# A fused gated-attention and rational-MLP kernel: the decay product of k moved to GpSimd, with a new order of work

## The chip, the cores and the metric

The kernel runs on one core of a Trainium2 chip. The core has a matrix engine (TensorE, PE in the profile, with its weight loads shown as PEld), VectorE (DVE), ScalarE (ACT), GpSimd (POOL) and a queue engine (SyncE, SP) that here only starts transfers. The engines run side by side, each through its own list of instructions in order, and wait for one another on semaphores. The metric is the time of one execution on the device, in microseconds (us); the median of several runs counts, and lower is better.

## The reference

Two stages follow each other. The first is a linear attention with a decay for each channel: a 48 x 48 state for each of 4 x 8 heads, over 768 steps. The second is an MLP whose nonlinearity is a rational function.

```python
def _attn_ref(q, k, v, f_logit):            # each (4, 8, 768, 48)
    f = 1.0 / (1.0 + np.exp(-f_logit))
    for t in range(S):
        state = f[:, :, t, :, None] * state + np.einsum('bhd,bhe->bhde', k[:, :, t], v[:, :, t])
        y[:, :, t] = np.einsum('bhd,bhde->bhe', q[:, :, t], state)

def _moe_ref(x, w_in, w_out, a, b):         # x (3072, 384), w_in (384, 2048), w_out (2048, 384)
    h = x @ w_in
    P = a[0] + a[1] * h + a[2] * h2 + a[3] * h3
    Q = 1.0 + np.abs(b[0]) * np.abs(h) + np.abs(b[1]) * h2
    return (P / (Q + 1e-06)) @ w_out
```

## The kernel before

The work is cut into 12 units, 256 tokens of one batch entry each: unit n takes token chunk n // 4 of batch entry n % 4. A unit passes through both stages. Nothing loops over the units in the code: one long string, `ORDER` (line 20), lists every step by a short name with its unit and its part, and the last loop of the kernel (L486) issues the steps in just that order. Since each engine runs its own instructions in the order in which they are issued, the string is the order of every engine's list. An `@` gives one of four PSUM slots to a step.

The steps of the attention, with the engine that runs each:

- `ld` loads f, k or q on SP's queue, v on GpSimd's (L114). `ef` and `ls` (ACT, L190 and L195) make the logarithm of the gate from f; `cs` (PE) sums it over the tokens of a piece; `A n x` (ACT, L221) exponentiates the sum, with x = 1 for k and x = 0 for q.
- `xa n x` (DVE, L227) is the decay product: k (x = 1) or q (x = 0) in fp32 times that factor, written as bf16 into the tile qkp. There are two qkp tiles, for units in turn. 128 partitions by 768 elements, all three operands in SBUF.
- `T` (PE) transposes both halves of qkp, and `Te` copies the result from PSUM to qkT: on ACT with an `s` behind it (L249), else on DVE (L251). `sc` (PE) makes the scores, `mk` (DVE, L272) multiplies them from PSUM with the mask.
- `vm` (GpSimd, L279) copies two strips of v, 128 elements a partition each. `kv`, `si` and `ae` make the new state in PSUM, `st` (DVE, L359) scales it from PSUM into SBUF. `yi` and `yb` (PE) make the output y, `ye` (ACT, L349) takes it to SBUF for the MLP. `kv` reads k's half of qkp too.

The steps of the MLP, on tiles of 16 blocks of 256 columns, often in halves (`0 8`, `8 16`) or quarters:

- `h` (PE, L368) multiplies with w_in, `hy` (ACT, L382) takes the result to SBUF. `sq` squares it (DVE, L386; `sa` is the same on ACT from PSUM), `ab` takes the absolute value into z (DVE, L394).
- Square and absolute value are added in one of three ways: on PE by `u` into PSUM, with the logarithm `ln` (ACT, L407) from there; in z on DVE by `zv` (L412); or in z by `zd`, a transfer that adds, issued on GpSimd's queue (L416). After `zv` and `zd` the logarithm is `lz` (ACT, L420). `ex` (ACT, L424) turns it into the reciprocal of Q.
- `p1`, `p2`, `pm` (DVE, L428, L433, L442) make the parts of P, added by `tv` on DVE (L450) or by `ta`, again a transfer that adds (GpSimd's queue, L446). `gm` (DVE, L454) multiplies with the reciprocal.
- `o` (PE, L462) multiplies with w_out, `oe` (ACT, the last one on DVE, L469) copies from PSUM, `so` stores on SP's queue. `wi` and `wo` load w_in and w_out in four slabs each on GpSimd's queue (L118, L124); `dz` are matmuls without use that fill PE's waits at the head.

`behind(i, mark)` (L477) makes an instruction wait for an earlier step that the dictionary `marks` holds by name.

Of the kernel before, what the change touches and what calls it, by code (L numbers as in the profile page):

```python
# [29 lines left out]
def kernel(  # L30
# [12 lines left out]
    nc = tc.nc  # L43
# [3 lines left out]
    HP = H // 2  # L47
# [14 lines left out]
    ld = ctx.enter_context(tc.tile_pool(name="ld", bufs=3))  # L62
# [30 lines left out]
    marks = {}  # L93

    def unit(n):
        if n not in units:
            c, b = divmod(n, B)
            units[n] = dict(c=c, b=b, qk=qkp[n % 2], ls=lsp[n % 2], vm=vmp[n % 2], st=states[b])
        return units[n]

    def slot(i, shape, dtype, name):
        return slots[i].tile(shape, dtype, name=name, tag="s")
# [114 lines left out]
    def A(n, x, a0=0, a1=HP):  # L217
        s = unit(n)
        t = A_sb[:, :, x, 2 * D * a0:2 * D * a1]
        src = s["cs", a0][:, :, 0:2 * D * (a1 - a0)]  # L220
        nc.scalar.activation(t, src, AF.Exp, scale=1.0 if x else -1.0)  # L221

    def xa(n, x, *args):
        s = unit(n)
        a0, a1 = args or (0, HP)
        hh = slice(2 * a0, 2 * a1)
        return nc.vector.tensor_mul(  # L227
            s["qk"][:, :, x, hh, 0:D],
            s["qk"[x]][:, hh].rearrange("p h i d -> p i h d"),
            A_sb[:, :, x].rearrange("p i (h d) -> p i h d", h=H)[:, :, hh])  # L230

    def T(n, *args):
        s = unit(n)
        a0, a1, sl = args if len(args) == 3 else (0, HP, args[0])
        t = s["tp", a0] = slot(sl, [P, 2, 2, HP, P], BF16, "tp")
        for x in (1, 0):
            for i in range(2):
                for p in range(a0, a1):
                    nc.tensor.transpose(t[:, x, i, p, :],  # L239
                                        s["qk"][:, i, x, 2 * p:2 * p + 2, :].rearrange("t h d -> t (h d)"), ident)  # L240

    def Te(n, *args):
        a0, a1 = [x for x in args if x != "s"] or (0, HP)
        s = unit(n)
        if "T" not in s:
            s["T"] = at.tile([P, 2, 2, HP, P], BF16, name="qkT")
        d, t = s["T"][:, :, :, a0:a1], s["tp", a0][:, :, :, a0:a1]
        if "s" in args:
            return nc.scalar.copy(d.bitcast(F32).rearrange("p x i a t -> p (x i) (a t)"),  # L249
                                  t.bitcast(F32).rearrange("p x i a t -> p (x i) (a t)"))  # L250
        return nc.vector.tensor_copy(d.rearrange("p x i a t -> p (x i) (a t)"),  # L251
                                     t.rearrange("p x i a t -> p (x i) (a t)"))
# [224 lines left out]
    def behind(i, mark):  # L477
        tc.add_manual_dep(i.ins, marks[mark].ins.name,
                          mybir.DependencyInfo(mybir.DependencyClass.Sync, mybir.DependencyReason.DATA),
                          reason="begins behind it")  # L480

    steps = dict(ld=load, wi=load_w_in, wo=load_w_out, ab_=load_ab, cu=const_u, ci=const_i, cm=const_m,
                 cz=const_z, fa=coef_a, fb=coef_b, fr=coef_r, ef=ef, ls=ls, cs=cs, A=A, xa=xa, T=T, Te=Te,
                 sc=sc, mk=mk, vm=vm, yi=yi, yb=yb, kv=kv, si=si, ye=ye, ae=ae, st=st, h=h, hy=hy, sq=sq, ab=ab, u=u, ln=ln,
                 zv=zv, zd=zd, sa=sa, lz=lz, ex=ex, p1=p1, p2=p2, pm=pm, ta=ta, tv=tv, gm=gm, o=o, oe=oe, so=store, dz=dz)
    for step in ORDER.replace("\n", ";").split(";"):  # L486
        if step.strip():
            name, *args = step.split()
            marks[".".join([name] + [x for x in args if x.isdigit()])] = steps[name](
                *(int(x.lstrip("@")) if x.lstrip("@").isdigit() else x for x in args))  # L490


# [1 line left out]
_INS = ['q', 'k', 'v', 'f_logit', 'moe_w_in', 'moe_w_out', 'moe_a', 'moe_b']  # L494
_OUTS = [((3072, 384), 'float32')]


# [23 lines left out]
```

## Time and profile before

| | us |
|---|---|
| median of 3 runs | 219.55 |
| the runs | 219.2, 221.58, 219.55 |
| the profiled execution | 218.93 |
| its span in the trace | 217.2 |

The profile shows one execution. Its span runs from the first instruction to the last; the execution's own time is a little longer than that. The page gives each engine's busy time and share of the span, the chain of work that ended last (followed back from the end, at each step to what released it), and groups of instructions by line, with the busy time and the mean length in ns of one behind a bar. A tile's name in a row is that of the program, with output before input. Further views, which the prediction quotes: busy time by stretches of the span, single instructions in order of time, and transfers by size with the time from issue to landing.

### The profile page before, as it was taken

Reading aid. Unit: us, or ns where it says so; the run is one execution under the profiler, and the core shown is the slowest. Engines: PE = TensorE matmul, PEld = TensorE weight load, DVE = VectorE, ACT = ScalarE, POOL = GpSimd, SP = SyncE. Lnnn points to the kernel's source line nnn. Section 1 sums busy time; section 2 is a strip of 40 time slices with the busy share of each in tenths; the row PEclk is TensorE's granted clock in tenths of the full one; section 3 lists DMA queues with packets and bytes.
Section 4 is the critical chain, followed back from the end, with each engine's and each line's share of the span. In section 5 each row is a group of like instructions: output and inputs, shape, how many; then the busy total and the mean of one; then the engine's idle time right before and its main releaser. Section 6 shows DMA issues by size and latency. Waiting matters only on the chain.

```text
span 217.2 us, 7159 instructions
## 1 busy us (share of the span) xinstructions
PE 203.3 (94%) x3164; PEld 140.2 (65%) x3171; DVE 202.9 (93%) x247; ACT 199.7 (92%) x209; POOL 90.2 (42%) x91
## 2 busy tenths in 40 slices
PE   6998989799799999999989999999999999999992
PEld 2456648458377658658758658668678577686551
DVE  4596999999999999999999999999999999999991
ACT  4734999999999999999999999999999999999990
POOL 5250072968146802014954205954332525433300
PEclk9999999999999999999999999999999999999999
DMA  5999999999897999958999997999789794999853
GB/s 141 244 228 206 216 249 203 204 251 213 122 240 145 236 232 279 150 100 195 196 232 214 210 250 182 181 231 219 152 170 227 140 155 83 174 185 189 157 213 145
DMA packets 60910, 42.13 MB, mean 194 GB/s; under 512 B 51152, under 2 KB 54992, under 8 KB 60880
## 3 DMA queue, kind: packets, MB, share of 16 engines
q0 software_dynamic: 21232, 22.81, 65.6%
q1 hardware_dynamic: 39360, 18.68, 34.0%
q8 instruction: 24, 0.39, 0.7%
q10 hardware_dynamic: 288, 0.20, 0.3%
q14 instruction: 6, 0.05, 0.1%
HBM read 25.17 MB, written 4.72 MB: 138 GB/s over the span
## 4 chain that ended last, share of the span: by engine, by line
DVE 36%; ACT 32%; DMA 15%; issue 7%; PE 7%; POOL 1%; POOLq 0%; DVEq 0%; ACTq 0%
ACT qi L424 8%; ACT hy L382 8%; ACT lq L420 6%; DVE h L386 6%; DVE scm L272 5%; DVE gall L454 5%; DMA w_in_sb<-in_moe_w_in_dram 4%; DMA kn<-in_k_dram 4%; DVE gall L442 4%; DVE z L394 3%; DVE qkp L227 3%; DVE gall L428 3%; DMA vn<-in_v_dram 3%; DMA z<-h 3%; DVE hy L433 3%
## 5 line engine op out<-in xcount | busy, mean ns | idle before, releaser
L462 PE MATMUL op<-w_out_sb,gall 128*128 128x384 bf16 x384 | 70.1, 326 | 0.4 <-ACT hy L382 0.4
L368 PE MATMUL hp<-xT,w_in_sb 128*128 128x256 bf16 x576 | 66.6, 273 | 1.6 <-ACT xT L349 0.9
L368 PEld LDWEIGHTS <-w_in_sb 128*128 128x128 bf16 x576 | 56.0, 98 | 11.8 <-issue 2.6
L279 POOL COPY vmp<-vn 128x128 bf16<-128x128 bf16 x24 | 41.9, 1758 | 31.8 <-DMA vn<-in_v_dram 27.8
L462 PEld LDWEIGHTS <-gall 128*128 128x128 bf16 x384 | 35.5, 98 | 23.7 <-DVE gall L454 1.0
L382 ACT CAST hy<-hp 128x1024 bf16<-128x1024 f32 x48 | 47.4, 1076 | 2.9 <-PE hp L368 2.9
L424 ACT ACTIVATE qi<-lq 128x2048 bf16<-128x2048 f32 (+1 forms) x26 | 46.9, 1845 | 0.0
L420 ACT ACTIVATE lq<-z 128x2048 f32<-128x2048 bf16 (+1 forms) x20 | 37.2, 1859 | 0.5 <-DMA z<-h 0.5
L446 POOL DMA_DIRECT2D gall<-hy x17 | 14.8, 925 | 50.6 <-PE hp L368 18.4
L416 POOL DMA_DIRECT2D z<-h x18 | 17.6, 1080 | 30.2 <-issue 10.4
L386 DVE TENSOR_TENSOR h<-hy 128x2048 bf16<-128x2048 bf16 (+1 forms) x26 | 27.3, 1059 | 2.7 <-ACT hy L382 2.7
L454 DVE TENSOR_TENSOR gall<-gall,qi 128x2048 bf16<-128x2048 bf16 (+1 forms) x26 | 29.4, 1139 | 0.2
L442 DVE TENSOR_TENSOR gall<-gall,h 128x2048 bf16<-128x2048 bf16 (+1 forms) x26 | 29.3, 1137 | 0.0
L272 DVE TENSOR_TENSOR scm<-sc,mask 128x1024 bf16<-128x1024 f32 x24 | 28.4, 1214 | 0.0
L221 ACT ACTIVATE A<-cs 128x768 f32<-128x768 f32 (+1 forms) x26 | 19.5, 813 | 0.4 <-DVE qkp L227 0.4
L394 DVE TENSOR_SCALAR z<-hy 128x2048 uint16<-128x2048 uint16 (+1 forms) x28 | 17.3, 625 | 0.2 <-ACT hy L382 0.2
L428 DVE TENSOR_SCALAR gall<-hy,a_sb 128x4096 bf16<-128x4096 bf16 (+1 forms) x14 | 17.1, 1218 | 0.0
L433 DVE TENSOR_SCALAR hy<-hy,a_sb 128x4096 bf16<-128x4096 bf16 (+1 forms) x14 | 16.6, 1187 | 0.0
L114 POOL DMA_DIRECT2D vn<-in_v_dram x12 | 14.1, 1175 | 0.7 <-PE y L286 0.7
L227 DVE TENSOR_TENSOR qkp<-kn,A 128x768 bf16<-128x768 f32 (+1 forms) x13 | 11.5, 888 | 1.9 <-ACT A L221 1.9
L349 ACT ACTIVATE xT<-y 128x768 bf16<-128x768 f32 x12 | 10.4, 868 | 3.0 <-PE y L286 3.0
L239 PE MATMUL tp<-ident,qkp 128*128 128x128 bf16 x192 | 12.8, 219 | 0.2
(70 smaller groups left out, 258.7 us busy)
## 6 DMA issues: line engine op xcount, KB each, us to landing
gall<-hy POOLq DMA_DIRECT2D x16, 512.0 KB, 6.6
z<-h POOLq DMA_DIRECT2D x15, 512.0 KB, 7.3
fn<-in_f_logit_dram SPq DMA_DIRECT2D x11, 384.0 KB, 8.9
kn<-in_k_dram SPq DMA_DIRECT2D x11, 384.0 KB, 9.5
qn<-in_q_dram SPq DMA_DIRECT2D x11, 384.0 KB, 6.8
out_dram<-osb SPq DMA_DIRECT2D x11, 384.0 KB, 4.2
vn<-in_v_dram POOLq DMA_DIRECT2D x12, 192.0 KB, 7.6
w_in_sb<-in_moe_w_in_dram POOLq DMA_DIRECT2D x4, 384.0 KB, 10.1
```

The source lines that it names most:

```text
L272: return nc.vector.tensor_mul(t, s["sc", g].rearrange("s r a i t -> s (r a) (i t)"), mb)
L279: nc.gpsimd.tensor_copy(s["vm"][:, :, :, 32 * x:32 * x + 16], src)
L368: nc.tensor.matmul(t[:, m - m0, :], w_in_sb[:, kk, m * P:(m + 1) * P], s["x"][:, kk].rearrange("p i j t -> p (i j t)"), start=(kk == 0), s ...
L382: nc.scalar.copy(fl(big(s, "hy", "hy", 3), m0, m1), fl(s["hp", m0], 0, m1 - m0))
L386: return nc.vector.tensor_mul(fl(big(s, "h2", "h2", 2), m0, m1), fl(s["hy"], m0, m1), fl(s["hy"], m0, m1))
L394: return nc.vector.tensor_scalar(fl(big(s, "z", "z", 2), m0, m1).bitcast(U16), fl(s["hy"], m0, m1).bitcast(U16), 0x7FFF, None, op0=ALU.bit ...
L420: nc.scalar.activation(fl(lq, m0, m1), fl(s["z"], m0, m1), AF.Ln, scale=regs[2], bias=1.0 + 1e-6)
L424: nc.scalar.activation(fl(qi, m0, m1), fl(lq, m0, m1), AF.Exp, scale=-1.0)
L428: return nc.vector.tensor_scalar(fl(big(s, "g", "gall", 3), m0, m1), fl(s["hy"], m0, m1), a_sb[:, 3:4], a_sb[:, 2:3], op0=ALU.mult, op1=AL ...
L442: return nc.vector.tensor_mul(fl(s["g"], m0, m1), fl(s["g"], m0, m1), fl(s["h2"], m0, m1))
L454: return nc.vector.tensor_mul(fl(s["g"], m0, m1), fl(s["g"], m0, m1), fl(qi, m0, m1))
L462: nc.tensor.matmul(s["op"][:, j, 0:DM], s["g"][:, m, P * j:P * j + P], w_out_sb[:, m, :], start=(s["on", j] == 1), stop=(s["on", j] == KF))
```

## The change

Three things are changed.

First, `xa` can run on GpSimd: with a `p` behind it, the product is the same multiplication on GpSimd instead of DVE, and is made to begin behind the mark `wide`. The loop that issues the steps sets that mark to the last DVE instruction so far of the kinds `sq`, `ab`, `p1`, `p2`, `pm`, `gm`, `zv`, `tv` and `xa`; these read and write SBUF alone.

```diff
     def xa(n, x, *args):
         s = unit(n)
-        a0, a1 = args or (0, HP)
+        pool = "p" in args
+        a0, a1 = [y for y in args if y != "p"] or (0, HP)
         hh = slice(2 * a0, 2 * a1)
-        return nc.vector.tensor_mul(
+        i = (nc.gpsimd if pool else nc.vector).tensor_mul(
             s["qk"][:, :, x, hh, 0:D],
             s["qk"[x]][:, hh].rearrange("p h i d -> p i h d"),
             A_sb[:, :, x].rearrange("p i (h d) -> p i h d", h=H)[:, :, hh])
+        if pool:
+            behind(i, "wide")
+        return i
...
     for step in ORDER.replace("\n", ";").split(";"):
         if step.strip():
             name, *args = step.split()
-            marks[".".join([name] + [x for x in args if x.isdigit()])] = steps[name](
+            i = marks[".".join([name] + [x for x in args if x.isdigit()])] = steps[name](
                 *(int(x.lstrip("@")) if x.lstrip("@").isdigit() else x for x in args))
+            if name in ("sq", "ab", "p1", "p2", "pm", "gm", "zv", "tv") or name == "xa" and "p" not in args:
+                marks["wide"] = i
```

Second, the whole `ORDER` is another one. The nine k products of units 3 to 11 (`xa 3 1` to `xa 11 1`) carry the `p`. Some steps take another form; all else is the same set of steps:

| step | before | after |
|---|---|---|
| k products on DVE / GpSimd (units 3 to 11) | 9 / 0 | 0 / 9 |
| `Te` of units 5 and 9 | ACT | DVE |
| `u` with `ln` (PE sum, quarters) | 11 | 3 |
| `zv` halves / quarters | 2 / 0 | 5 / 2 |
| `lz` halves / quarters | 17 / 3 | 20 / 5 |
| `zd` halves / quarters | 15 / 3 | 15 / 3 |
| `tv` halves / quarters | 6 / 3 | 6 / 2 |
| `ta` halves / quarters | 16 / 1 | 16 / 2 |
| warming matmuls (`dz`) | 31 | 24 |

With unit 0's two half copies, four `Te` steps now run on DVE.

Third, all steps stand in another place. At the head, q and k of unit 0 are loaded ahead of f of unit 1 and of v; the decay products of unit 0 begin with q; the exponentials and logarithms of units 1 and 2 stand between the steps of unit 0; w_in's slabs come from the first to the last. The nine products stand where DVE's list has masks and states next. The list around four of them, in the new order (each excerpt is a part of the one long line):

```
p1 1 0 16; ae 2; A 3 1; st 2 0; sc 2 1 @2; sc 2 0 @1; zd 1 8 16; A 3 0; ls 4; si 2 1; xa 3 1 p; mk 2 0; ex 0 8 16; yb 2 0 2 @0; yi 2 1; mk 2 1; yb 2 2 4; xa 3 0; vm 3 0; st 2 1; cs 4 @1; ye 2 s; wo 0 4; wo 4 8; T 3 @2
...
zv 2 0 8; mk 4 1; xa 5 1 p; ef 6; ae 4; o 1 0 8 12; mk 4 0; si 4 0; st 4 0; o 1 0 4 8; ld 7 q; lz 2 0 8; ex 2 0 8; o 1 1 8 12; gm 2 8 16
...
sq 6 8 16; xa 8 1 p; mk 7 1; st 7 0; lz 5 8 16; ex 5 8 16; o 4 1 8 12; mk 7 0; o 4 1 0 4; ld 10 k; ab 6 8 16
...
xa 11 0; mk 10 0; lz 8 0 8; mk 10 1; o 7 1 8 12; xa 11 1 p; vm 10 1; kv 10 @1; ab 9 8 16
```

At the tail the copy `oe 9` stands behind the last `ex`, and the stores of units 6, 7 and 8 are issued together.

2 lines of the change are left out of this document (1 added, 1 removed).

## The prediction

> **What bounds the kernel now.** I read the page's totals first, then the chain that ended last.
>
> ```profile
> span 217.2 us, 7159 instructions
> ...
> PE 203.3 (94%) x3164; PEld 140.2 (65%) x3171; DVE 202.9 (93%) x247; ACT 199.7 (92%) x209; POOL 90.2 (42%) x91
> ...
> DVE 36%; ACT 32%; DMA 15%; issue 7%; PE 7%; POOL 1%; POOLq 0%; DVEq 0%; ACTq 0%
> ```
>
> Three engines are busy for over 90% of the span, but the chain runs through VectorE (DVE) and ScalarE (ACT): 36% and 32%, with 7% on TensorE (PE). So work taken off PE alone is worth little. The busy times in stretches of 10 us come next (columns: stretch, length, then busy time and instructions of PE, PE's weight loads, DVE, ACT and GpSimd, the granted clock, DMA share, GB/s).
>
> ```profile
> 0.00:10.00 10.00, 8.02 (x32) 3.23 (x33) 4.75 (x28) 6.38 (x11) 3.88 (x15) 1.00 0.96 187
> 10.00:20.00 10.00, 8.95 (x195) 5.40 (x194) 7.98 (x14) 3.48 (x5) 3.78 (x6) 1.00 1.22 222
> 20.00:30.00 10.00, 9.89 (x193) 7.12 (x194) 8.97 (x13) 8.78 (x11) 2.16 (x4) 1.00 1.26 227
> ...
> 210.00:217.20 7.20, 3.14 (x19) 1.40 (x16) 2.06 (x4) 1.97 (x3) 0.00 (x0) 1.00 0.29 109
> sum 217.20, PE 203.29 PEld 140.16 DVE 202.89 ACT 199.68 POOL 90.18; mean PE 9.24 PEld 6.37 DVE 9.22 ACT 9.08 POOL 4.10
> ```
>
> DVE idles 217.20 - 202.89 = 14.3 us: 5.25 + 2.02 + 1.03 = 8.3 in the first 30 us, 7.20 - 2.06 = 5.1 in the last stretch, and so only 0.9 in the 180 us between. ACT idles 17.5, of which 3.62 + 6.52 + 1.22 = 11.4 at the head, 5.2 at the tail, 0.9 between. In the middle both are full: a microsecond of DVE work saved there shows in the end only if ACT gives up as much, and a stall of either shows whole. The clock is 1.00 in every row.
>
> **The change, part by part.** The rows for each kind of instruction (busy time and mean ns of one behind the bar):
>
> ```profile
> L420 ACT ACTIVATE lq<-z 128x2048 f32<-128x2048 bf16 x17 | 33.8, 1991 | 0.5 <-DMA z<-h 0.5
> L272 DVE TENSOR_TENSOR scm<-sc,mask 128x1024 bf16<-128x1024 f32 x24 | 28.4, 1214 | 0.0
> ...
> L249 ACT COPY qkT<-tp 128x1024 f32<-128x1024 f32 x11 | 11.9, 1077 | 0.0
> ...
> L407 ACT ACTIVATE lq<-u 128x1024 f32<-128x1024 f32 x11 | 11.2, 1041 | 0.0
> L359 DVE TENSOR_TENSOR state<-sv,alast 128x384 bf16<-128x384 f32 x20 | 11.0, 548 | 0.1
> ...
> L227 DVE TENSOR_TENSOR qkp<-kn,A 128x768 bf16<-128x768 f32 x11 | 10.4, 948 | 0.0
> ...
> L402 PE MATMUL u<-z,ident 128*128 128x512 bf16 x22 | 6.5, 379 | 0.4
> ...
> L420 ACT ACTIVATE lq<-z 128x1024 f32<-128x1024 bf16 x3 | 3.3, 1108 | 0.0
> ...
> L412 DVE TENSOR_TENSOR z<-z,h 128x2048 bf16<-128x2048 bf16 x2 | 2.4, 1220 | 0.0
> L450 DVE TENSOR_TENSOR gall<-gall,hy 128x1024 bf16<-128x1024 bf16 x3 | 2.1, 685 | 0.0
> ...
> L251 DVE COPY qkT<-tp 128x1024 bf16<-128x1024 bf16 x2 | 1.3, 687 | 0.0
> ```
>
> and of single instructions in order of time (start, length), first DVE's, then ACT's last ones:
>
> ```profile
> 13.47 2.36 DVE L272 TENSOR_TENSOR scm<-sc,mask 128x1024 bf16<-128x1024 f32 x2
> ...
> 45.14 1.33 DVE L428 TENSOR_SCALAR gall<-hy,a_sb 128x4096 bf16<-128x4096 bf16 x1
> 46.39 1.21 DVE L454 TENSOR_TENSOR gall<-gall,qi 128x2048 bf16<-128x2048 bf16 x1
> 47.52 0.95 DVE L227 TENSOR_TENSOR qkp<-kn,A 128x768 bf16<-128x768 f32 x1
> ...
> 51.53 1.34 DVE L433 TENSOR_SCALAR hy<-hy,a_sb 128x4096 bf16<-128x4096 bf16 x1
> ...
> 69.38 0.68 DVE L394 TENSOR_SCALAR z<-hy 128x2048 uint16<-128x2048 uint16 x1
> ...
> 71.42 0.94 DVE L394 TENSOR_SCALAR z<-hy 128x2048 uint16<-128x2048 uint16 x1 [0.22 <-ACT hy L382]
> ```
>
> ```profile
> 209.75 1.06 ACT L424 ACTIVATE qi<-lq 128x1024 bf16<-128x1024 f32 x1
> 210.71 0.78 ACT L469 COPY osb<-op 128x768 f32<-128x768 f32 x1
> 213.18 0.48 ACT L469 COPY osb<-op 128x384 f32<-128x384 f32 x1 [1.69 <-PE op L462]
> ```
>
> *DVE.* Nine k products (units 3 to 11, L227) leave: 9 x 0.948 = 8.53 us. The new order also reassigns other work. Two full copies of qkT (units 5 and 9) come over from ACT; the row is for half the size (0.687), so one costs between 1.22 (a 2048-element DVE row, L412) and 2 x 0.687 = 1.37; I take 1.30, as the source is that row's: 2.60. Additions of z on DVE (L412) go from two of 2048 to five of 2048 and two of 1024: 3 x 1.220 + 2 x 0.685 = 5.03 (L450 for the small ones, the same operation and size). One addition of 1024 at L450 goes: 0.69. Net 8.53 + 0.69 - 2.60 - 5.03 = 1.59 us less, in three instructions fewer. Neighbours overlap in these rows: the one begun at 46.39 lasts 1.21 and the next begins at 47.52, an overlap of 0.08. So 1.6 - 3 x 0.08 = 1.35, say 1.4 us.
>
> *ACT.* Two copies of 1.077 and eight logarithms from PSUM of 1.041 go: 10.48. Three logarithms from z of 1.991 and two of 1.108 come: 8.19. Net 2.29 less, in five instructions fewer; ACT's rows overlap by 209.75 + 1.06 - 210.71 = 0.10 each, so 1.8 us.
>
> *PE* loses the eight u sums, four matmuls each: at most 32 x 0.379 = 12.1 us of busy time, off the chain. Seven warming matmuls go too, in the head, where PE waits anyhow. I count both at nothing: DVE's and ACT's full middle hides PE there, and where PE was the wait, the chain's 7% (15 us, most of it matmuls that stay) bounds it.
>
> DVE gives the smaller relief, so the span gets 1.4 us, if the products cost DVE nothing from GpSimd. That is the term to look at. The trace has no product on GpSimd, but it has its copies of 128 elements (L279):
>
> ```profile
> 9.30 0.28 POOL L279 COPY vmp<-vn 128x128 bf16<-128x128 bf16 x1 [5.16 <-DMA vn<-in_v_dram]
> ...
> 13.48 0.30 POOL L279 COPY vmp<-vn 128x128 bf16<-128x128 bf16 x1
> ...
> 45.96 5.81 POOL L279 COPY vmp<-vn 128x128 bf16<-128x128 bf16 x1 [1.89 <-issue]
> ...
> 71.84 1.87 POOL L279 COPY vmp<-vn 128x128 bf16<-128x128 bf16 x1
> ```
>
> The copy at 9.30 took 0.28 with DVE waiting. The one at 13.48 took 0.30 while DVE ran the mask product (L272) from PSUM at its usual rate: they go side by side. The one at 45.96 took 5.81, while DVE ran p1, gm, xa and pm back to back from SBUF, and ended as p2 began at 51.53. So GpSimd's read waits for DVE's SBUF work, up to twenty times its own length, and DVE was hardly held: the worst I find is z at 71.42, 0.94 against 0.68 for its like at 69.38, with a copy waiting from 71.84 on and a transfer's issue before it. For a DVE wait behind a long GpSimd read the trace has no row; it is bounded below by nothing (side by side) and above by the product's whole length each time.
>
> The new wait is made for this: each product begins behind the last SBUF operation of DVE, and next on DVE stand PSUM operations, masks (L272) and states (L359). From the new order the cover, with 1.13 (1.21 - 0.08) for a mask and 0.47 for a state: mask, mask, state in either order for units 3 and 5 to 9, 2.73 each; one state more for unit 4, 3.20; two masks alone for units 10 and 11, 2.26. The length of a product: not under DVE's own 0.95; 768/128 = 6 copies' worth is 6 x 0.28 = 1.7; twice that, if each of its two operands is read at the copy's rate, is 3.4. I take 1.7, as a copy's 0.28 has its start in it six times over, and a second operand is read instead. With some 0.2 to start behind a wait, 1.9 fits into every cover; for places where a copy or two (0.3 each) stands ahead of it on GpSimd I leave 0.4 in all.
>
> The Trainium skill, "GPSIMD Engine Reference", section 3.1, gives 4497 ns for a two-input fp32 operation of 2048 elements and keeps "use DVE for elementwise" as the rule; an estimate by that page is 768/2048 of it, 1.69 us, and the sum would stay as it is. Its page "SBUF — State Buffer", section "Who interferes with whom", says that the shared port pair is held for the whole instruction and whoever comes second fully blocks. The 5.81 us agree for GpSimd as the second; no row shows DVE as the second, and by that rule a product that starts late is paid by DVE, which is the first rival.
>
> *What stands behind the product on GpSimd:* copies of v, and the issues of the z and gall additions. From the list, a z addition of the middle units becomes ready 9.8 us of ACT work or more ahead of its logarithm, except for unit 2 (7.1) and the last two units (4.6 to 8.5).
>
> ```profile
> z<-h POOLq DMA_DIRECT2D x15, 512.0 KB, 7.3
> ...
> w_out_sb<-in_moe_w_out_dram POOLq DMA_DIRECT2D x4, 384.0 KB, 10.7
> ```
>
> Against 7.3 from issue to landing (half-size pieces of the last unit move half as much) a product's 2 us is covered in the middle, and unit 2 and the end have nothing to spare. Two w_out loads stand behind the first product as well: from their place to the first output matmul lie about 9 us of ACT work, against 10.7 to land. So PE may wait 1 to 2 us there; it holds eight u sums less, and I charge nothing.
>
> *Head.* f for unit 1 moves behind k and q of unit 0, so that these land earlier, and ef and ls of units 1 and 2 fill ACT's waits; but the first w_in slab is still issued behind the copy at 9.30, and the first h waits for it. I count 0, within 0.5. *Tail:*
>
> ```profile
> 213.69 0.56 DVE L469 COPY osb<-op 128x384 f32<-128x384 f32 x1 [2.08 <-DMA out_dram<-osb]
> ```
>
> Behind the last ex (209.75) ACT has one osb copy (0.78) and then waits 1.69 for PE; DVE's last copy waits for a store. The new order puts the copy of unit 9 there too, which takes up to 0.87 of ACT work from before the last ex, but its store joins the last ones. With DVE as the bound I count 0.3.
>
> Sum: 217.2 - 1.4 + 0.4 - 0.3 = 215.9. The profiled run took 218.93, 1.73 outside its span: 217.6. The median shown (219.55; runs 219.2 and 221.58) is 0.62 above the profiled run; one late run raises such a median, so I add half of it: **217.9 us**.
>
> **Rivals.** *The product overruns its cover.* It reads at the two-operand rate, or starts late behind copies that DVE's SBUF run held up, and DVE's next SBUF operation waits. With length plus start x, DVE loses 6(x - 2.73) + 2(x - 2.26) + (x - 3.20) where positive. At x = 2.9 that is 1.0 + 1.3 = 2.3 us, which undoes the gain; from x = 3.15 (2.5 + 1.8 = 4.3 us in place of the 0.4) the kernel is over 1% slower; at 3.6 (3.4 + 0.2) it is 5.2 + 2.7 + 0.4 = 8.3, so 217.9 - 0.4 + 8.3 = 225.8. For it: the 5.81 us, and the new order has long SBUF runs ahead of units 5 and 6. Against: copies beside a mask run at full speed. That the product then frees nothing on DVE is the far end of the same case. Slower: 222 to 226.
>
> *A transfer becomes the wait*: w_out, unit 2's z, or the last z pieces arrive 1 to 2 us late and PE or ACT stands still. 219.2 to 221.5.
>
> *More than the work goes.* With DVE and ACT both lighter, PE's u sums gone and tail copies moved, the 0.9 us of idle in the middle, the tail's whole 0.87 and 0.5 to 1 of the head go as well: 215 to 216.7.
>
> **How the numbers follow.** About 1% (2.2 us) is what a measurement can tell from no change: below 217.35 is faster, above 221.75 slower. The forecast, with its own range of 216.7 to 219.2 (Te and the cover's leftover either way, half the median's offset), gets 0.46, of which 0.18 lies below 217.35. The rival of lighter ends gets 0.18, the late transfer 0.12, the overrun 0.24. Faster 0.18 + 0.18 = 0.36; same 0.28 + 0.12 = 0.40; slower 0.24. Range: to 215.2 at the low end leaves out few hundredths; to 222.6 reaches into the overrun and leaves out some 0.17.
>
> **What would show it.** DVE's busy time near 201.5 and ACT's near 197.9; each GpSimd product lasting 1.5 to 2.3 us, with a mask beside it and the next SBUF row on DVE at its usual length. An overrun shows as a gm, sq or tv of 2 us or more right after the masks, or as a product that spans an SBUF run. A late transfer shows as DMA in ACT's or PE's waits. DVE busy near 201 with idle in the middle would say that the work sum was right and a wait ate it; the head's idle of DVE away from 8.3 by over 1 us, that I misjudged the reordering.

## The result, and the profile after

| | before | after |
|---|---|---|
| median, us (6 runs each) | 220.00 | 226.90 |
| the runs, us | 218.78 to 221.64 | 226.35 to 228.28 |
| profiled execution, its span | 218.93, 217.2 | 226.64, 224.9 |
| VectorE busy, idle (profile) | 202.89, 14.3 | 202.26, 22.6 |
| ScalarE busy, idle (profile) | 199.68, 17.5 | 199.83, 25.1 |

The ratio of the times is 1.0311, with a 95% interval of 1.0251 to 1.0371: slower, and above the whole range of the prediction. (Ratios, here and below, leave out runs that came out over 1.5% longer than the fastest of the same kernel, which medians and ranges still contain; five of e5's six did, and it has no ratio.) The page of the kernel after (busy time, the clock by fortieths of the span, the chain that ended last):

```profile
span 224.9 us, 7099 instructions
...
PE 202.5 (90%) x3132; PEld 138.8 (62%) x3132; DVE 202.3 (90%) x244; ACT 199.8 (89%) x204; POOL 90.9 (40%) x101
...
PEclk9999999889999999976999999999999999999999
...
DVE 29%; ACT 23%; PE 21%; issue 10%; DMA 7%; POOL 4%; SPq 4%; POOLq 0%; ACTq 0%; DVEq 0%
```

VectorE (DVE) has hardly less work than before, but 8.3 us more idle time, and PE, on 7% of the chain before, is on 21% of it now. The clock, 1.0 throughout before, has two dips. Cut into stretches (columns: stretch, length, then busy time and instructions of PE, PE's weight loads, DVE, ACT and GpSimd, the clock, DMA share, GB/s), the kernel after:

```profile
0.00:30.00 30.00, 24.38 (x420) 14.31 (x421) 20.84 (x52) 19.59 (x27) 10.31 (x24) 1.00 1.19 205
30.00:93.00 63.00, 57.27 (x889) 40.73 (x888) 61.65 (x66) 60.80 (x65) 26.73 (x25) 0.97 1.05 208
93.00:112.00 19.00, 15.11 (x209) 11.00 (x207) 13.81 (x14) 13.26 (x13) 10.93 (x8) 0.82 0.97 195
112.00:205.00 93.00, 90.30 (x1527) 64.00 (x1525) 91.86 (x94) 91.50 (x88) 39.02 (x40) 1.00 0.88 166
205.00:224.90 19.90, 15.40 (x95) 8.78 (x93) 14.09 (x22) 14.69 (x15) 3.88 (x5) 0.99 0.78 200
```

and the kernel before in the same cuts, except that its last stretch begins 5 us earlier:

```profile
0.00:30.00 30.00, 26.86 (x416) 15.75 (x419) 21.70 (x54) 18.64 (x26) 9.82 (x24) 1.00 1.15 212
30.00:93.00 63.00, 58.53 (x943) 41.71 (x931) 62.74 (x67) 62.60 (x69) 31.45 (x23) 1.00 1.12 206
93.00:112.00 19.00, 18.52 (x360) 12.88 (x358) 19.00 (x20) 19.00 (x20) 10.91 (x9) 1.00 0.87 184
112.00:200.00 88.00, 86.29 (x1418) 62.74 (x1404) 87.49 (x92) 87.50 (x85) 36.31 (x35) 1.00 0.98 186
200.00:217.20 17.20, 13.09 (x77) 7.09 (x75) 11.96 (x18) 11.94 (x13) 1.69 (x2) 1.00 0.64 173
```

DVE's idle time is the length less its busy time. Of the 8.3 us more, 19.00 - 13.81 = 5.2 lie between 93 and 112 us, where before there was none; 21.70 - 20.84 = 0.9 in the first 30 us; 62.74 - 61.65 = 1.1 between 30 and 93 us; the rest in the last two stretches. The main loss is one place. The moved instructions themselves are close to what was planned (groups by line and shape; busy time, mean ns of one):

```profile
L228 POOL TENSOR_TENSOR qkp<-kn,A 128x768 bf16<-128x768 f32 x9 | 16.9, 1881 | 7.0 <-ACT qi L428 3.0 <-DVE qkp L228 1.6 <-PE sc L268 1.2
...
L255 DVE COPY qkT<-tp 128x2048 bf16<-128x2048 bf16 x2 | 2.4, 1210 | 0.0
```

Nine products on GpSimd last 1.88 us each on average, where the prediction took 1.7 and 0.2 to start. A full copy of qkT on DVE lasts 1.21, where it took 1.30.

Now the place, engine by engine in order of time (start, length). GpSimd, with one undisturbed product first:

```profile
42.35 1.82 POOL L228 TENSOR_TENSOR qkp<-kn,A 128x768 bf16<-128x768 f32 x1
...
93.37 0.85 POOL L420 DMA_DIRECT2D z<-h  x1 [7.93 <-ACT h L394]
93.94 2.15 POOL L228 TENSOR_TENSOR qkp<-kn,A 128x768 bf16<-128x768 f32 x1
95.71 3.73 POOL L283 COPY vmp<-vn 128x128 bf16<-128x128 bf16 x1
95.94 4.75 POOL L420 DMA_DIRECT2D z<-h  x1
```

DVE over the same time, with its k product of unit 1 at the head ahead of it:

```profile
20.67 0.96 DVE L228 TENSOR_TENSOR qkp<-kn,A 128x768 bf16<-128x768 f32 x1 [2.12 <-DMA kn<-in_k_dram]
...
93.83 2.34 DVE L276 TENSOR_TENSOR scm<-sc,mask 128x1024 bf16<-128x1024 f32 x2
96.09 1.21 DVE L454 TENSOR_TENSOR gall<-gall,hy 128x2048 bf16<-128x2048 bf16 x1
...
99.23 1.33 DVE L432 TENSOR_SCALAR gall<-hy,a_sb 128x4096 bf16<-128x4096 bf16 x1
...
110.88 1.22 DVE L390 TENSOR_TENSOR h<-hy 128x2048 bf16<-128x2048 bf16 x1 [5.19 <-ACT hy L386]
```

and PE:

```profile
95.64 0.24 PE L290 MATMUL y<-scm,vn 64*32 64x128 bf16 x4
99.49 0.30 PE L290 MATMUL y<-scm,vmp 64*32 64x128 bf16 x4 [3.61 <-POOL vmp L283]
...
102.71 1.91 PE L243 MATMUL tp<-ident,qkp 128*128 128x128 bf16 x16
```

Read the three together. The transfer z (L420) at 93.37 had waited for ACT; the product of unit 6 stands behind it, begins at 93.94 beside DVE's masks (L276, 93.83) and runs to 96.09, so it stays inside their cover of 2.34 us. But behind the product on GpSimd stands the small copy `vm 5 0` (L283), and it comes to its turn just as DVE leaves the masks and goes into its next run of operations from SBUF (96.09 to 100.5). The copy, 0.3 us long by itself, ends only at 99.44 (95.71 + 3.73), when DVE has passed from rows with two operand tiles to p1 (99.23). PE needs its strip for the output y of unit 5: after y's first matmuls from vn (95.64) it stands still for 3.61 us, until 99.49. Its clock then is low, 0.50 from 99 to 104 us: 16 transposes at 102.71 take 1.91 us, against 1.06 in e4 below, where the clock stays at 1.00. The waits, summed up by who waits for whom (total, times, longest):

```profile
ACT xT L353 <- PE y L290: 5.8, 5, 3.7
DVE h L390 <- ACT hy L386: 5.8, 2, 5.2
...
PE y L290 <- POOL vmp L283: 3.6, 1, 3.6
```

PE's 3.6 us, and the slow matmuls behind them, delay the w_in matmuls of unit 5, ACT's copies of their results, and so DVE's square behind them: DVE has worked off what it has by 105.69 (its row at 104.48 lasts 1.21) and is idle for 5.19 us.

### The profile page after: what moved, and what is told of

Its sections match the earlier page's. It is cut to its first block, busy times and chain, and to the rows that moved or that the text cites. A ratio compares the mean times of both kernels' runs of the same rounds, so it can differ in the third digit from the quotient of the medians.

```text
span 224.9 us, 7099 instructions
## 1 busy us (share of the span) xinstructions
PE 202.5 (90%) x3132; PEld 138.8 (62%) x3132; DVE 202.3 (90%) x244; ACT 199.8 (89%) x204; POOL 90.9 (40%) x101
## 4 chain that ended last, share of the span: by engine, by line
DVE 29%; ACT 23%; PE 21%; issue 10%; DMA 7%; POOL 4%; SPq 4%; POOLq 0%; ACTq 0%; DVEq 0%
ACT hy L386 8%; PE hp L372 7%; PE op L466 6%; DVE h L390 6%; DMA kn<-in_k_dram 5%; DVE scm L276 5%; ACT lq L424 4%; DVE gall L458 4%; SPq L114 4%; DVE gall L432 4%; PE y L290 3%; ACT qi L428 3%; DVE gall L446 3%; DVE z L398 3%; ACT A L221 2%
## 5 line engine op out<-in xcount | busy, mean ns | idle before, releaser
L466 PE MATMUL op<-w_out_sb,gall 128*128 128x384 bf16 x384 | 71.1, 328 | 0.5 <-DVE gall L458 0.4
L428 ACT ACTIVATE qi<-lq 128x2048 bf16<-128x2048 f32 (+1 forms) x26 | 46.2, 1806 | 0.1
L424 ACT ACTIVATE lq<-z 128x2048 f32<-128x2048 bf16 (+1 forms) x25 | 43.9, 1771 | 0.2 <-DMA z<-h 0.2
L420 POOL DMA_DIRECT2D z<-h x18 | 22.0, 1221 | 51.2 <-DVE z L398 21.9
L283 POOL COPY vmp<-vn 128x128 bf16<-128x128 bf16 x24 | 23.2, 1032 | 24.8 <-DMA vn<-in_v_dram 23.4
L390 DVE TENSOR_TENSOR h<-hy 128x2048 bf16<-128x2048 bf16 (+1 forms) x26 | 27.4, 1055 | 6.0 <-ACT hy L386 5.8
L450 POOL DMA_DIRECT2D gall<-hy x18 | 16.0, 890 | 36.8 <-DVE hy L437 24.0
L276 DVE TENSOR_TENSOR scm<-sc,mask 128x1024 bf16<-128x1024 f32 x24 | 28.6, 1213 | 0.7 <-PE sc L268 0.7
L228 POOL TENSOR_TENSOR qkp<-kn,A 128x768 bf16<-128x768 f32 x9 | 16.9, 1881 | 7.0 <-ACT qi L428 3.0
L398 DVE TENSOR_SCALAR z<-hy 128x2048 uint16<-128x2048 uint16 (+1 forms) x28 | 17.6, 630 | 0.1
L114 POOL DMA_DIRECT2D vn<-in_v_dram x12 | 16.0, 1354 | 0.0
L243 PE MATMUL tp<-ident,qkp 128*128 128x128 bf16 x192 | 13.9, 227 | 2.2 <-DVE qkp L228 1.9
L290 PE MATMUL y<-scm,vmp 64*32 64x128 bf16 x384 | 12.3, 232 | 3.6 <-POOL vmp L283 3.6
```

The costliest lines, as they stand in the source:

```text
L114: eng.dma_start(out=s[what][:, hh].rearrange("p h i d -> p h (i d)"), in_=src[s["b"], hh, t0:t0 + NT, :].rearrange("h (p i) d -> p h (i d) ...
L276: return nc.vector.tensor_mul(t, s["sc", g].rearrange("s r a i t -> s (r a) (i t)"), mb)
L390: return nc.vector.tensor_mul(fl(big(s, "h2", "h2", 2), m0, m1), fl(s["hy"], m0, m1), fl(s["hy"], m0, m1))
L398: return nc.vector.tensor_scalar(fl(big(s, "z", "z", 2), m0, m1).bitcast(U16), fl(s["hy"], m0, m1).bitcast(U16), 0x7FFF, None, op0=ALU.bit ...
L424: nc.scalar.activation(fl(lq, m0, m1), fl(s["z"], m0, m1), AF.Ln, scale=regs[2], bias=1.0 + 1e-6)
L428: nc.scalar.activation(fl(qi, m0, m1), fl(lq, m0, m1), AF.Exp, scale=-1.0)
```

## The experiments

Each experiment starts from the kernel after, unless it says otherwise; "before" is the kernel before, run on the same chip. The edits are to the list `ORDER`.

**e1: the copy ahead of the product.**

```diff
-vm 5 1; ex 2 8 16
+vm 5 1; vm 5 0; ex 2 8 16
...
-si 5 1; vm 5 0; yb 5 0 2
+si 5 1; yb 5 0 2
```

> One step is moved: the copy vm 5 0 goes from behind the product of unit 6 to right behind vm 5 1, ahead of it, on GpSimd's list. Theory (a missed cover): in the changed kernel the copy began at 96.09, as the product ended and DVE went from masks to SBUF work, waited to 99.44, and PE waited 3.6 us for it; DVE then idled 5.2 us between 93 and 112. With the copy done early, PE's wait for vmp and DVE's 5.2 us go, the clock stays at 1.00 there, and the time is 220.5 to 222.5. Rival (the products as such, or the new order as a whole, cost the time in many places): the wait at unit 5 shows slack elsewhere, and the time stays above 225.

Measured: 221.55 (220.37 to 222.83), ratio 1.0089 (1.0061 to 1.0117). One moved copy of 128 elements a partition takes the ratio from 1.0311 to 1.0089: 0.0222 x 219.65 = 4.9 us of the 6.8 lost. The stretch that had lost 5.2 us is full again, at full clock:

```profile
93.00:112.00 19.00, 18.06 (x287) 12.30 (x284) 19.00 (x21) 19.00 (x20) 9.58 (x9) 1.00 1.03 201
```

So the late copy is the main cause. 0.9% stay open. Two places are left in e1's profile: the head, with 9.3 us of DVE's idle time in the first 30 us (8.3 before), to which e5, e11 and e13 go, and a second dip of the clock at 45 us, to which e10 and e12 go.

**e2 and e3: all nine products back on DVE, or only the one of unit 6.** The order stays that of the kernel after; the `p` is taken away from all nine `xa n 1 p`, or from `xa 6 1 p` alone.

> The nine k products go back to DVE at the same places of the new order; nothing else changes. Theory (products cheap, one copy caught behind one of them): DVE gets 9 x 0.87 = 7.8 us of work back, the wait for vm 5 0 goes with its 5 us, since GpSimd is free when the masks of unit 5 begin; the sum is +2 to +3, 228 to 230. Rival (the products cost more than they free): the time falls below 225.

> Only the product of unit 6 goes back to DVE; the copy vm 5 0 keeps its late place. Theory (it is the product ahead of it that makes the copy miss the masks): the copy runs during the masks in about 0.3 us, PE's wait for vmp falls under 0.5 us, and the time is 5 us less plus 0.9 for the product on DVE: 221.5 to 223.5. Rival (the copy's late place in the list alone is the fault, whatever is ahead): the copy still lasts over 2 us, and the time stays at 226 to 228.

Measured: e2 228.49, ratio 1.0368 (1.0321 to 1.0416); e3 221.92, ratio 1.0102 (1.0070 to 1.0134). In e3, taking the one product off GpSimd cures the place about as well as moving the copy does (1.0102 against 1.0089), though the copy keeps its late place: neither the late place nor the product ahead of it does the harm alone. The copy then runs under the masks in both; in e2 and in e3 GpSimd's rows are

```profile
97.77 0.58 POOL L283 COPY vmp<-vn 128x128 bf16<-128x128 bf16 x1
```

```profile
94.29 0.60 POOL L283 COPY vmp<-vn 128x128 bf16<-128x128 bf16 x1
```

0.6 us instead of 3.7. In e2 that stall is gone, but DVE carries 208.6 us of work, and the kernel is 228.49 - 221.55 = 6.9 us slower than e1, which has the same order with the copy right: nine products times 0.87 (0.95 less the overlap of 0.08) are 7.8. (In the profiles DVE's busy time differs by 208.6 - 202.3 = 6.3. e2's profile also lost clock at the head, 0.89 over 30 us, so not all of the 6.9 need be the products.) The offload is worth about what it weighs in this order; but the order without it has 208.6 - 202.9 = 5.7 us more DVE work than the kernel before, which the offload first has to pay back.

**e4: PE kept busy during the wait.** Fourteen warming matmuls stand where PE waits for the copy; the copy stays late.

```diff
-vm 5 0; yb 5 0 2
+vm 5 0; dz 14 @3; yb 5 0 2
```

> 14 warming matmuls of 0.21 us are put into PE's list right ahead of the y matmuls of unit 5 that wait for the copy; they write a free PSUM slot. The copy's wait stays. Theory A (half of the loss at unit 5 is the clock): in the changed kernel the 16 transposes behind the wait took 1.91 us for 1.05, and the clock was 0.75 from 100 to 110; with PE kept busy the clock stays at 1.00 and the time falls by about 2 us, to 224 to 225.5. Theory B (the wait alone costs it, the clock only shows it): within 0.5 us of the changed kernel, 226.5 to 227.5.

Measured: 225.84, ratio 1.0284 (1.0245 to 1.0322), the profiled run 224.58 against 226.64. PE's rows:

```profile
96.39 3.18 PE L214 MATMUL warm<-Ui 128*128 128x512 bf16 x14 [0.51 <-DVE scm L276]
...
101.50 1.06 PE L243 MATMUL tp<-ident,qkp 128*128 128x128 bf16 x16
```

The wait is the same, but filled, and the transposes behind it take 1.06 us where they took 1.91. DVE is busy for 16.29 us from 93 to 112 us, against 13.81. So in the profiles about half of the 5.2 us lost there is the wait, and half the slow clock after it. By the ratios the gain is only 0.0027 x 219.65 = 0.6 us, and the two intervals overlap, so the times do not show a gain: the median lies between what the two theories gave, and the three other runs were granted a lower clock (0.975 to 0.984) than the profiled one (0.989). That the filled wait keeps the clock there is shown by this profile alone.

**e6: the products without their wait.** From e1, `behind(i, "wide")` is taken away: each product begins as soon as its factor and its tile are there.

```diff
         if pool:
-            behind(i, "wide")
+            pass
```

> On top of the moved copy, the products lose their wait for DVE's last SBUF operation; they begin when their inputs are there and GpSimd comes to them. Theory A (GpSimd is the one that waits, as its copies do): products that come early wait through SBUF runs, their rows get longer than 1.8 us, DVE's rows keep their lengths, and the time stays within 0.7 us of the run with the moved copy (221.55). Theory B (by the page SBUF - State Buffer of the Trainium skill, whoever is second blocks fully): some products get in between two SBUF operations, and DVE shows rows longer by up to 1.8 us in their place; with four or more of nine, the time rises by 3 to 8 us.

Measured: 228.63, ratio 1.0426 (1.0387 to 1.0466), 0.0337 x 219.26 = 7.4 us more than e1, with DVE's busy time at 208.3 against 202.3. DVE's rows at two of four places that lose 6.6 us together:

```profile
45.20 2.22 DVE L228 TENSOR_TENSOR qkp<-qn,A 128x768 bf16<-128x768 f32 x1
...
125.74 3.62 DVE L432 TENSOR_SCALAR gall<-hy,a_sb 128x4096 bf16<-128x4096 bf16 x1
```

and GpSimd's at the second:

```profile
126.12 2.15 POOL L228 TENSOR_TENSOR qkp<-kn,A 128x768 bf16<-128x768 f32 x1
```

The second instruction, p1, is 1.34 us long elsewhere. Here it starts at 125.74, the product at 126.12, and p1 ends at 129.36 (125.74 + 3.62), 2.28 us later than it should. At 45.20 q's product (0.95 us elsewhere) is behind a k product begun at 44.41 and lasts 2.22. So theory B holds: DVE is held until the product is done. At all four places (the others are a z addition at 110.73 and q's product at 177.01) its instruction ends 0.8 to 1.1 us behind the product's end. The prediction had weighed this rule of the Trainium skill ("SBUF — State Buffer", section "Who interferes with whom") without a row that shows DVE as the second; here is the row, and it agrees. One difference: p1 was issued 0.38 us first and still lost, so the order of the starts in the trace did not tell here who comes first.

**e7 and e8: GpSimd products in the order of the kernel before.** e7 puts the `p` on the nine products where they stood. e8 does so for units 3 and 5 alone, and moves these two to where masks come next on DVE:

```diff
-xa 3 1; 
...
-u 1 4 8 @0; mk 2 1;
+u 1 4 8 @0; xa 3 1 p; mk 2 1;
...
-xa 5 1; 
...
-mk 4 1; so 0 0 2 s
+xa 5 1 p; mk 4 1; so 0 0 2 s
```

> The old order, step for step, but with its nine k products of units 3 to 11 on GpSimd, each behind DVE's last SBUF operation, at their old places, where DVE's list mostly has SBUF operations next. Theory (a product is cheap only under masks): the products wait through SBUF runs as the copies did, 2 to 6 us each; the transposes behind them come late, DVE's busy time falls by 7 to 8 us but idle takes it back, and the time is 220 to 228. Rival (a product on GpSimd is cheap anywhere): rows of 1.8 to 2.2 us throughout, and the time falls towards ACT's limit, by 1 to 3 us, to 216.5 to 218.5.

> The old order with two k products (units 3 and 5) on GpSimd, moved to where DVE's list has two masks next; the factor that they need is there by then. Nothing else changes. Theory (a product under masks costs DVE nothing): DVE's busy time falls by 1.7 us, ACT's does not; the time falls by 0.4 to 1.2 us against the kernel before. Rival (ACT at 199.7 us holds the end): no change within 0.4 us.

Measured: e7 232.24, ratio 1.0594 (1.0550 to 1.0639), the slowest of all and above what was expected; e8 219.62, ratio 1.0000 (0.9971 to 1.0030). In e7, by groups:

```profile
L390 DVE TENSOR_TENSOR h<-hy 128x2048 bf16<-128x2048 bf16 x18 | 25.3, 1415 | 1.6 <-ACT hy L386 1.5
L228 POOL TENSOR_TENSOR qkp<-kn,A 128x768 bf16<-128x768 f32 x9 | 19.4, 2161 | 6.0 <-issue 2.5 <-ACT hy L386 2.4 <-DVE gall L432 1.2
...
L398 DVE TENSOR_SCALAR z<-hy 128x2048 uint16<-128x2048 uint16 x20 | 17.0, 856 | 0.3 <-ACT hy L386 0.3
```

DVE's z (L398) lasts 0.86 on average where it lasted 0.71, its squares (L390) 1.42 instead of 1.23, its q products 1.33 instead of 0.96, and GpSimd's products 2.16. In that order SBUF work follows the product on DVE, and both lose: DVE's busy time rises to 207.2 instead of falling by 7 to 8. PE waits 6.9 us in sum for the products ahead of `kv` and 3.2 ahead of `T`. The expectation had only GpSimd wait, and for longer: no product lasts over 2.9 us. In e8 the two products take 1.83 and 1.82. The first begins at 44.03, behind an issue and 1.7 us after the masks, and reaches past them into p1, which takes 1.86 where it took 1.33 before:

```profile
45.09 1.86 DVE L432 TENSOR_SCALAR gall<-hy,a_sb 128x4096 bf16<-128x4096 bf16 x1
```

The second stays under its masks and disturbs nobody. DVE's busy time falls by 0.8, to 202.1, about half of the 1.7 expected, and the time doesn't move at all, as the rival had it: ACT still has 199.7 us to do. That ACT is what keeps the time is argued from this; e9 tries it.

**e9: the freed time given to ACT's work.** From e8, the two quarters of unit 4 that ACT squares (`sa`) go to DVE.

```diff
-sa 4 0 4; 
...
-sa 4 4 8; 
...
-ab 4 0 8; ae 5
+ab 4 0 8; sq 4 0 8; ae 5
```

> The old order with two k products (units 3 and 5) on GpSimd under masks, and one more step: the two squares of unit 4 that ACT takes from PSUM (1.07 us each) become one square on DVE (1.22). Theory (with DVE relieved by the products, ACT held the end): ACT gets about 1.9 us less, DVE in all 0.6 less than the kernel before, and the time falls by 0.5 to 1.0 us, to a ratio of 0.995 to 0.998. Rival (some wait at the head or tail holds the end): ratio 0.999 to 1.003.

Measured: 221.63 (219.87 to 222.65), ratio 1.0071 (1.0036 to 1.0106). A miss: ACT's busy time falls to 198.3, but from 50 to 93 us it now waits:

```profile
50.00:93.00 43.00, 41.25 (x642) 29.15 (x642) 42.17 (x44) 41.38 (x45) 15.80 (x12) 1.00 1.01 199
```

41.38 of 43 us, against 42.68 in e8. So 1.3 us of the work taken off ACT came back as waiting there. It is PE that ACT waits for, 0.38 us for an `h` and then for the state's matmul:

```profile
90.79 0.18 ACT L359 ACTIVATE alast<-sv 128x8 f32<-128x8 f32 x1 [0.91 <-PE sv L348]
```

That matmul starts at 90.42, and at 90.46 in e8: the squares on ACT had filled this wait, and taking them away only showed it. DVE, which now has the square ahead of its state, comes to the state at 92.35 instead of 91.33. DVE's busy time is 203.2 us against 202.1; that this makes the whole rise of the time is not shown. Less ACT work at this place does not shorten the time; whether it would at another was not tried.

**e5 and e11: k of unit 1 earlier at the head.** In the kernel after, DVE waits 2.12 us at 20.67 for k of unit 1, behind f of units 1 and 2 on SP's queue. e5 is e1 with k moved ahead of f of unit 2; e11 is e10 (below) with this and `ef 2` moved behind `A 1 1`, so that ACT should not wait for the f that is now later.

```diff
-ld 1 f; ld 2 f; wi 0 4
+ld 1 f; ld 1 k; wi 0 4
...
-A 0 0 2 4; ld 1 k; xa 0 0 2 4
+A 0 0 2 4; ld 2 f; xa 0 0 2 4
```

> On top of the moved copy (vm 5 0 ahead), two loads change places on SP's list: k of unit 1 goes ahead of f of unit 2. Theory (the head lost by the new order of loads): in the changed kernel k of unit 1 landed at 20.6, DVE waited 2.12 us for it, and DVE had done 20.84 us of work by 30 us against 21.70 before. With the swap DVE's work by 30 us rises to 21.5 or more and the time falls by 0.5 to 1 us against the run with the moved copy alone (221.55), to 220.6 to 221.0. Rival (the head is bound by the loads' sum, or by the first products): f of unit 2 comes late in its place and the time stays within 0.4 us, or rises.

> On top of that, the head: k of unit 1 is loaded ahead of f of unit 2, as in the run that became slower, but ef of unit 2 now stands on ACT's list behind both decay factors of unit 1, so that a late f holds nothing up. Theory (the swap failed since ACT waited in order for f of unit 2): DVE's work by 30 us rises from 20.7 to 21.3 or more and the time falls by 0.3 to 1 us against the run without the swap. Rival (the head is bound by the amount loaded, in any order): DVE's work by 30 us stays under 20.9 and the time is within 0.4 us or higher.

Measured: e5 222.94 to 228.0, median 227.26; e11 227.46, ratio 1.0342 (1.0284 to 1.0399). Both are misses. DVE has 13.9 us (e5) and 13.4 us (e11) of work done by 30 us, against 20.7 in e1, and PE's clock is 0.66 from 20 to 30 us in both. In e5, whose profiled run took 227.37 (the one run at 222.94 has no profile), k comes early, but f of unit 2 is late, and ACT's list has it ahead of the factor of unit 1:

```profile
20.11 0.84 ACT L190 ACTIVATE fn<-fn 128x768 f32<-128x768 f32 x1 [6.55 <-DMA fn<-in_f_logit_dram]
20.86 1.49 ACT L221 ACTIVATE A<-cs 128x768 f32<-128x768 f32 x2
```

In e11 the same f, still ahead of the first `ye` (whose row is L353, at 23.44), holds up h, and DVE stands:

```profile
21.82 0.84 ACT L190 ACTIVATE fn<-fn 128x768 f32<-128x768 f32 x1 [4.78 <-DMA fn<-in_f_logit_dram]
```

```profile
28.08 0.69 DVE L390 TENSOR_TENSOR h<-hy 128x1024 bf16<-128x1024 bf16 x1 [7.92 <-ACT hy L386]
```

In these two tries one late transfer was only exchanged for another, and how much of the loss is the wait and how much the low clock behind it stays open. The order as changed costs DVE about 1 us at the head, and both others cost more.

**e10: fewer PE waits at unit 3.** The second dip of the clock, at 45 us, comes after two waits of PE: for the state of unit 2, which stands behind p1 on DVE, and for the masks. e10 is e1 with that p1 behind the masks.

```diff
-p1 1 0 16; ae 2
+ae 2
...
-yb 2 2 4; xa 3 0
+yb 2 2 4; p1 1 0 16; xa 3 0
```

> On top of the moved copy (221.55), one DVE step changes its place: p1 of unit 1 (1.34 us) goes from ahead of the state and the two masks of unit 2 to behind them. Theory (a second place of the same kind): in the changed kernel PE waited for that state and those masks (1.21 and 0.81 us at 42.7 and 43.9), its clock fell to 0.83 from 40 to 50, and ACT idled 1.56 us there; with the state 1.3 us earlier the clock stays at 1.00, ACT's idle there falls under 0.5, and the time falls by 0.8 to 1.8 us, to 219.7 to 220.8. Rival (the delay is made up for later by full engines): within 0.5 us of 221.55.

Measured: 222.07, ratio 1.0111 (1.0052 to 1.0171): no gain. PE's rows there in e1, and then in e10:

```profile
43.29 0.32 PE L348 MATMUL sv<-state,ident 128*128 128x384 bf16 x1 [1.48 <-DVE state L363]
...
47.58 1.38 PE L243 MATMUL tp<-ident,qkp 128*128 128x128 bf16 x16
```

```profile
42.17 0.32 PE L348 MATMUL sv<-state,ident 128*128 128x384 bf16 x1 [0.23 <-DVE state L363]
...
46.25 1.92 PE L243 MATMUL tp<-ident,qkp 128*128 128x128 bf16 x16
```

The wait for the state fell from 1.48 to 0.23 us (the one for the masks stayed at 0.81), and yet the transposes last 1.92 us. In this profile shorter waits alone did not keep the clock.

**e12 and e13: PE filled at unit 3, then at the head too.** e12 is e1 with five warming matmuls at the two waits; e13 adds five more at the head, where PE waits for unit 0's k product.

```diff
-ls 4; si 2 1; xa 3 1 p
+ls 4; dz 2 @0; si 2 1; xa 3 1 p
...
-ex 0 8 16; yb 2 0 2 @0
+ex 0 8 16; dz 3 @0; yb 2 0 2 @0
...
-wi 0 4; dz 6 @3; T 0 0 2 @3
+wi 0 4; dz 11 @3; T 0 0 2 @3
```

> The version with copy vm 5 0 ahead, plus five warming matmuls on PE at unit 3, two ahead of the state term of unit 2 and three ahead of y of unit 2: the two places at which PE waits 1.48 and 0.81 us in that version, and behind which the granted clock shows 0.71 and 0.50. They fill at most 1.4 of the 2.3 us. Theory A: the rest of that version's loss, 0.9% over the kernel before, is half this clock dip: the clock over 40 to 50 us is 0.95 or more, the 16 transposes of unit 3 last 1.06 to 1.15 (1.38 there), ACT waits 1 us less there, and the time is 220.3 to 220.9 (ratio 1.003 to 1.006). Theory B: ACT waits there for the masks on DVE, which the clock does not move, or the dip begins already in the 0.9 us that stays empty: 221.2 to 222 (ratio 1.007 to 1.011).

> The version of the run before (copy vm 5 0 ahead, five warming matmuls at unit 3) plus five more warming matmuls at the head, ahead of the first transposes of unit 0: there PE waits for the k product of unit 0, 0.80 us in the profile of e1 and 2.36 us in that of the run before, where the granted clock fell to 0.52 behind it, the masks came 2.2 us later than in e1, and VectorE had 18.0 us of work done by 30 us (20.7 in e1). Five last about 1.1 us. Theory A: this dip is what separates the seven of its eleven runs at a clock of 0.981 to 0.988 (median 221.9) from the four at 0.997 to 0.999 (220.0 to 221.0): most runs then show 0.995 or more and the median is 219.9 to 220.6 (ratio 1.001 to 1.005). Theory B: the late landing itself, not the clock, costs the time: the clock is 0.995 or more and the median stays at 221.2 to 222.

Measured: e12 221.61 (219.98 to 224.37), ratio 1.0068 (1.0038 to 1.0097); e13 221.60 (219.21 to 224.69), ratio 1.0047 (1.0000 to 1.0094). In stretches, e1, e12 and e13:

```profile
0.00:30.00 30.00, 24.14 (x413) 13.88 (x415) 20.68 (x51) 19.65 (x27) 10.04 (x24) 1.00 1.18 208
...
40.00:50.00 10.00, 7.47 (x154) 5.22 (x154) 10.00 (x11) 7.87 (x11) 5.12 (x6) 0.83 1.19 232
```

```profile
0.00:30.00 30.00, 24.17 (x333) 13.89 (x335) 18.00 (x50) 17.17 (x26) 10.50 (x24) 0.89 1.17 201
...
40.00:50.00 10.00, 8.28 (x203) 5.82 (x202) 10.00 (x12) 9.24 (x12) 4.64 (x5) 1.00 1.09 226
```

```profile
0.00:30.00 30.00, 24.99 (x422) 14.50 (x424) 20.78 (x52) 19.86 (x28) 10.25 (x24) 1.00 1.18 206
...
40.00:50.00 10.00, 8.48 (x165) 6.03 (x163) 10.00 (x12) 9.02 (x11) 5.49 (x6) 1.00 1.19 230
```

At unit 3 theory A is right about the clock: with the waits filled it is 1.00 in place of 0.83, in e12 and e13, and ACT is busy for 9.24 and 9.02 us of 10 instead of 7.87. The time did not follow. The profiled run of e12 lost its clock at the head: 0.89, and DVE has 18.00 us done by 30 us. e12's runs divide by their granted clock: four of eleven, at 0.997 to 0.999, took 219.98 to 220.99, those at 0.981 to 0.988 took 221.26 and more. e13 keeps the clock in its profile, which took 220.47, but its runs scatter as much: at 0.996 to 1.0 they took 219.2 to 222.1. Ratios of 1.0089, 1.0068 and 1.0047 go down as the fills come in, but neighbours overlap, and which of e13's theories holds stays open. No version beat the kernel before; e8 equals it, and e13's interval reaches 1.0000 at its lower end only.

## Why the prediction was wrong, point by point

*The failed step* is in the paragraph on what stands behind the product on GpSimd. It names "copies of v, and the issues of the z and gall additions", works out the additions and w_out, and leaves the wait of a copy *behind* the product unpriced. The 0.4 us left in all was for a copy *ahead* of the product that delays it. The price was in rows that the prediction quoted: a copy took 5.81 us while DVE ran back to back from SBUF. A product put behind the last SBUF operation uses up the cover; a copy that had its turn there before is pushed out of it, into DVE's next SBUF run. That is a rival that was not on the list: it adds nothing to DVE's own rows, where the overrun was looked for, but costs time through PE. Its general sign, DVE's work as summed with idle time in the middle, was on the list and came: 202.3 us, and 5.2 idle at one place. e1 and e3 show it from two sides: 4.9 us, and 0.0209 x 219.65 = 4.6. e1's 221.55 is still 3.6 above the 217.9 forecast; what follows names where the rest may lie, and does not prove it.

*The product and its cover.* Right: 1.81 to 1.85 in seven places, 2.04 and 2.15 behind an issue, against covers of 2.26 and more; no gm, sq or tv of 2 us beside them. The estimate of 1.69 from the figure of the Trainium skill ("GPSIMD Engine Reference", section 3.1) was 7% short of 1.81. The overrun, the main rival for "slower", did not happen; that the ratio (1.0311 x 219.55 = 226.4) lands next to its 222 to 226 is chance. The late transfer did not happen either: ACT waits 0.2 us for z in all (0.5 before), PE not at all for w_out.

*DVE "hardly held" by a GpSimd read* was the reading of rows in which GpSimd always came second. e6 and e7 correct it: up to 2.3 us a time. The prediction's bounds for such a wait, nothing to the product's whole length, about hold: 2.28 for p1 beside a product of 2.15.

*The work.* DVE's rows fell by the 1.4 us summed (k products 10.4 to 2.0, z additions 2.4 to 7.6, copies of qkT 1.3 to 3.8, small gall additions 2.1 to 1.4), but its busy time by 0.6 only. The rows count the overlap of neighbours twice, and where a wait lies between two rows there is none; DVE's waits go from 9 to 16. That this is the difference was not tried. ACT was to get 1.8 us less and has the same busy time, 199.8. Even in e8, which has neither the late copy nor the new order, 0.8 us less on DVE moved the time by nothing, so the sum would probably have been too hopeful without any stall.

*The head* was counted at 0 within 0.5, and DVE has 0.9 us less done by 30 us; k of unit 1, late behind two f loads, is its longest wait there (2.12 us), but no run moved k without loss elsewhere. PE's warming matmuls taken out there were counted at nothing; the profiles of e2 and e12, with a clock of 0.89 over the head, speak against that, and the kernel after, with 1.00 there, does not. *The tail* was given 0.3: DVE works 2.04 us in the last 7.2, and worked 2.06 before, so none of it came.

*PE's u sums at nothing* because DVE's and ACT's full middle hides PE: that argument asked only whether PE is busy too long. What decided was PE standing still, where it passes on its wait at once and then runs slow. What the missing u sums did by themselves was not tried.

## What to carry to other kernels

When a long GpSimd operation is put under the one stretch in which DVE leaves it alone, list what was using that stretch: put small GpSimd copies that someone waits for ahead of it, and check that what stands behind it has a cover of its own. Do not count freed time on one of two full engines as time gained: 0.8 us on DVE gave nothing (e8), and taking work off the other engine gave nothing either where that work had filled a wait for a third (e9). Price a wait of PE at its length and the slow matmuls after it (about as much again in e4's profile), and where it can't be taken away, fill it.

## What the runs showed of the hardware

GpSimd and DVE hold each other up in both directions over operations from SBUF: GpSimd's copy of 0.3 us took 3.73 behind DVE (after), DVE's p1 of 1.34 took 3.62 around a product of 2.15 (e6); beside masks and states, which read PSUM, seven of nine products take 1.81 to 1.85 and two masks their usual 2.34.

PE's granted clock falls after waits: to 0.50 from 99 to 104 us behind 3.61 us, with 1.91 us for the transposes in place of 1.06. At unit 3 waits of 1.48 and 0.81 us, 0.3 us of matmuls between them, were enough for 1.38 (e1), and waits of 0.23, 0.81 and 0.33 for 1.92 (e10), while in the kernel after 1.21 and 0.81 left them at 1.06 and the low clock (0.50 from 44 to 46 us) fell on the matmuls before. The Trainium skill ("TensorE: Matmul & The Clock Gate", part 1) has the clock halved after an idle window of about 3.4 us that runs freely. The 3.61 us agree with it. The waits at unit 3 are shorter than that window, and the clock is 0.50 behind them all the same; no run here shows why.
